# Two transpose banks kept through the attention, and a pair's sum and casts one step later

## The chip, the cores and the metric

The kernel runs on one core of a Trainium2 chip. The metric is device time in microseconds (us), the median of several runs. Its engines are called PE (TensorE matmul; PEld is its weight load), DVE (VectorE), ACT (ScalarE), POOL (GpSimd) and SP (SyncE, which issues most DMAs).

## The reference

Attention with hashed buckets over 2 x 8 heads of 768 positions and 64 dimensions, then two feed-forward blocks on the 1536 x 512 result:

```python
q_bits = (einsum(q, proj) > 0); k_bits = (einsum(k, proj) > 0)   # 6 bits each
mask = q_bucket[..., :, None] == k_bucket[..., None, :]          # same 6 bits
scores = where(mask, scale * q @ k.T, -1e9)
attn = softmax(scores)
x = attn @ v                                  # then (1536 x 512)
x = (sigmoid(x @ w_gate) * (x @ w_val)) @ w_out     # d_ff 1536
h = x @ w_in                                  # d_ff 2048
out = (h * cos(h)) @ w_out2
```

## The kernel before

Nearly every product is made of float32 values split in a rounded part and the rest, in two or three matmuls. `attention()` runs first and `moe()` behind it.

The attention is a software pipeline over steps `g`. A step is one head and one tile of 128 queries, so a head has T = 6 steps and all 16 heads have NG = 96. The stages of one step lie several steps apart: `scores` (PE, L483 and L486: the code bits and the values of q and k) writes the scores `s`; `rowmax` (DVE, L500) makes `mn`; `expo` (ACT, L507) makes the exponentials `p`, and after every third step `sm` (L517); `coef` (DVE, L533) makes the reciprocal `r`; `norm` (POOL, L540) scales `p`. LAG = 7 steps behind, `ptrans` (PE, L556) transposes blocks `t` of `p`, two to a step; `phi` (ACT, L561) rounds each to `ph`, `plo` (DVE, L566) makes the rest `pl`, and `pv` (PE, L576 with `ph`, L577 with `pl`) sums six of them into the output `o` of half a head. `fin_act` (ACT, L586) copies that one bank `o` to `e`; this comes every third step, and the first `pv` of the next half head can only follow it.

Two heads make a pair with 128 rows. When its last half is copied, DMAs bring its halves to the right partitions (L597 to L600), and then the pair is finished: `fin_sum` adds the two halves in `ef` (L613), `fin_hi` rounds the sum to the input `xy` of the feed-forward block (ACT, L625 or L642), `fin_lo` makes the rest (POOL, L646). For the first six pairs the sum is split: `fin_wide` adds 512 columns on DVE and rounds them on ACT (L625), while POOL adds the other 256, which `fin_hi` rounds (L642). SUM_AT, HIGH_AT and LOW_AT say how many steps after the copy of the pair's last half this is done (the sum on DVE and its cast one step after SUM_AT).

The next heads are prepared beside that: `trans` transposes q and k (`pt`, PE L302; rounded into `x`, or copied to `xf` by ACT, L319), `bits_steps` multiplies them by the projection in six matmuls (`pb`, PE L368), and `code` (DVE, L353) makes the code bits `bf`, which DMAs (L390) bring into the operands of `scores`.

The order on every engine is the order in which the code calls these functions, since the whole lies in a manual schedule: the lists ORDER, ROOM (steps with a wide sum), LAST and FILL (the steps before the first transposes of `p`) name the stages of a step in their order. PREP stands for what was put down for this step in advance (`todo`), S for the scores of a later step, FIN for the copy of `o`, SUM for `fin_wide`.

PSUM has eight banks. Scores take four; at the start another two hold a third buffer for scores, and two (`ps_u`) hold transposes and bits in turn. At step 5 `change_banks` gives these four back and makes three banks for `t`, `pt` and `pb` (`ps_t`) and one for `o` (`ps_o`). The feed-forward blocks begin with `pg`, `pv` and `ph` (L864), of which some fill PE at the end of the attention.

Of the kernel before, what the change touches and what calls it, by code (L numbers as in the profile page):

```python
# [9 lines left out]
F32 = mybir.dt.float32  # L10
# [6 lines left out]
PSUM = bass.MemoryType.PSUM  # L17

P = 128

ORDER = (
    "Tb LOa COEF NRM PVb EXP Ta MIN LATE W HIb PVa PREP S FIN HIa Tc PVaF LOb".split()
)
# [2 lines left out]
)  # L26
LAST = ["COEF", "NRM"] + [name for name in ORDER if name not in ("COEF", "NRM")]
FILL = "COEF NRM MIN EXP LATE W PREP S".split()

LOAD_AT = {"q": -17, "k": -19, "v": -6}  # L30
TRANS_AT = (-12, -10)
BITS_AT = -8
VALUES_AT = (-3, -1)

SUM_AT, HIGH_AT, LOW_AT = 3, 5, 5
BIG = float(2.0**34)
CUT = float(2.0**30)
INV2PI = 1.0 / (2.0 * math.pi)
# [5 lines left out]
def lsh_attention_glu_moe_cos_moe(  # L44
# [14 lines left out]
    B, H, S, D = q.shape  # L59
# [7 lines left out]
    HS = S // 2  # L67
# [168 lines left out]
    def attention():  # L236
        nonlocal done
        parts = None
        with ExitStack() as st:
# [4 lines left out]
            tiny = st.enter_context(tc.tile_pool(name="tiny", bufs=3))  # L244
            work = st.enter_context(tc.tile_pool(name="work", bufs=2))
            ps_s = st.enter_context(tc.tile_pool(name="ps_s", bufs=1, space=PSUM))
            first = ExitStack()
            ps_f = first.enter_context(tc.tile_pool(name="ps_f", bufs=1, space=PSUM))
            ps_t = first.enter_context(tc.tile_pool(name="ps_u", bufs=2, space=PSUM))
            ps_o = None  # L250

            def change_banks():
                nonlocal ps_t, ps_o
                first.close()
                s_ps.pop()
                ps_t = st.enter_context(tc.tile_pool(name="ps_t", bufs=3, space=PSUM))
                ps_o = st.enter_context(tc.tile_pool(name="ps_o", bufs=1, space=PSUM))

            NG = NH * T
            heads = {}  # L260
# [28 lines left out]
            def trans(hd, half, fast=False):  # L289
                hh = heads.setdefault(hd, {})  # L290
                if half == 0:
                    hh["x"] = [
                        prep.tile([P, T, P], F32R, tag=f"x{i}", name=f"x{i}_{hd}", bufs=2)
                        for i in range(2)
                    ]
                    for nm in ("q1", "k1", "q2", "k2"):
                        hh[nm] = prep.tile([P, T, P], F32R, tag=nm, name=f"{nm}_{hd}")
                xh, xl = hh["x"]
                sl = slice(3 * half, 3 * half + 3)
                pt = ps_t.tile([P, 3, P], F32, tag="t", name=f"pt{hd}{half}")  # L300
                for i in range(3):
                    nc.tensor.transpose(pt[:, i, :], raw[hd][:, 3 * half + i, :], ident)  # L302

                def high():
                    nc.scalar.activation(xh[:, sl, :], pt, AF.Copy, scale=qscale)

                def low():
                    nc.vector.scalar_tensor_tensor(
                        out=xl[:, sl, :],
                        in0=pt,  # L310
                        scalar=qscale,
                        in1=xh[:, sl, :].bitcast(F32),
                        op0=ALU.mult,
                        op1=ALU.subtract,
                    )

                def whole():
                    xf = work.tile([P, 3, P], F32, tag="xf", name=f"xf{hd}{half}", bufs=2)
                    nc.scalar.activation(xf, pt, AF.Copy, scale=qscale)  # L319
                    return xf  # L320

                def rest_of(xf):
                    nc.gpsimd.tensor_tensor(
                        out=xl[:, sl, :], in0=xf, in1=xh[:, sl, :].bitcast(F32), op=ALU.subtract
                    )

                def both():
                    xf = whole()
                    nc.gpsimd.tensor_scalar(
                        out=xh[:, sl, :], in0=xf, scalar1=1.0, scalar2=1.0, op0=ALU.mult, op1=ALU.mult  # L330
                    )
                    rest_of(xf)
                    if half == 1 and hd > 2:
                        place(hd, 0)
                        place(hd, 1)

                if hd == 1 and half == 0:
                    return high, lambda: rest_of(whole())
                return (high, low) if fast else both

            def place(hd, i):
                lo, hi = slice(0, D), slice(D, P)
                if i == 0:
                    raw.pop(hd)
                hh = heads[hd]
                for nm, rows, part in (
                    (("q2", slice(32, 96), lo), ("k1", lo, hi), ("q1", lo, lo), ("k1", hi, hi)),
                    (("k2", slice(32, 96), hi), ("q1", hi, lo)),
                )[i]:
                    nc.sync.dma_start(hh[nm][rows].bitcast(F32), hh["x"][i][part].bitcast(F32))  # L350
# [9 lines left out]
                )  # L360

            def bits_steps(hd):
                pb = ps_t.tile([P, HS], F32, tag="t", name=f"pb{hd}")
                hh = heads[hd]
                n = 0
                for low, half in ((0, 0), (0, 1), (1, 0), (1, 1)):
                    for i in range(2 - low):
                        nc.tensor.matmul(  # L368
                            pb,
                            pw[:, i, slice(0, P) if half else slice(D, D + P)],  # L370
                            hh["x"][low][:, 3 * half : 3 * half + 3, :],
                            start=(n == 0),
                            stop=(n == 5),
                        )
                        n += 1
                    yield pb
# [24 lines left out]

            def first_head():
                split = [trans(0, half, fast=True) for half in range(2)]
                hh = heads[0]
                xh, xl = hh["x"]
# [144 lines left out]

            def ptrans(w):
                u, j = divmod(w, T)
                pt = ps_t.tile([P, 3, P], F32, tag="t", name=f"t{w}")
                for i in range(3):
                    pv_ = p_t[3 * u + i].rearrange("p a s -> p (a s)")
                    nc.tensor.transpose(pt[:, i, :], pv_[:, j * P : (j + 1) * P], ident)  # L556
                pt_t[w] = pt
# [90 lines left out]
            LAG = 7  # L648
# [10 lines left out]
            for hd in range(2, NH):  # L659
                s1 = T * hd  # L660
                if hd > 2:
                    for nm in "qk":
                        at(max(s1 + LOAD_AT[nm], -2) if hd > 3 else 2, lambda hd=hd, nm=nm: load(hd, nm))
                if hd % 2 == 0:
                    at(max(s1 + LOAD_AT["v"], 8), lambda hd=hd: load(hd, "v"))
                for half in range(2):
                    if hd > 2:
                        at(
                            max(s1 + TRANS_AT[half], 7),
                            lambda hd=hd, half=half: trans(hd, half),  # L670
                        )
                    else:
                        at(3 * half - 1, lambda half=half: second_head(half))
                if hd > 2:
                    at(s1 + BITS_AT, lambda hd=hd: bits(hd))
                at(s1 + VALUES_AT[hd % 2], lambda hd=hd: values(hd))
# [12 lines left out]
            at(4, lambda: two_more())  # L689
            at(5, lambda: bits(2, split2[0])())  # L690
            at(5, change_banks)

            def second_head(half):
                if half == 0:
                    return trans(2, 0)
                high, low = trans(2, 1, fast=True)

                def upper():
                    high()
                    low()  # L700
                    place(2, 0)
                    place(2, 1)
                    split2.append(bits_steps(2))
                    next(split2[0])

                return upper
# [11 lines left out]
            with tc.manual_schedule(  # L718
# [35 lines left out]
                scores(0)  # L754
                scores(1)
                split1 = bits_steps(1)
                for _ in range(2):
                    next(split1)
# [10 lines left out]
                for g in range(NG + LAG + 2):  # L769
# [32 lines left out]
                    if g == LAG - 2:  # L802
                        at(g, lambda: ptrans(0))
                        at(g, lambda: ptrans(1))
# [21 lines left out]
                        "SUM": (g in wide, lambda: wide.pop(g)()),  # L826
                        "HIa": (0 <= wa + 2 < NW, lambda: phi(wa + 2)),
                    }
                    steps = ORDER if LAG - 1 <= g != NG else LAST if g == NG else FILL
                    for name in ROOM if g in wide else steps:  # L830
                        on, fn = ops[name]
                        if on:
# [5 lines left out]
    def moe():  # L838
        with ExitStack() as st:
# [172 lines left out]
            with tc.manual_schedule(  # L1012
# [8 lines left out]
                for n, (kind, l, f, c) in enumerate(items):  # L1021
# [7 lines left out]
                    else:  # L1029
                        (layer_out1 if l == 1 else layer_out2)(c, f)  # L1030

    attention()
    moe()

# [40 lines left out]
```

## Time and profile before

| what | value |
|---|---|
| median of 3 runs | 799.45 us (799.36 to 799.46) |
| the profiled execution | 800.5 us |
| span of the profiled execution | 798.7 us |
| granted TensorE clock | full (all 40 slices) |
| PE, PEld busy | 99%, 85% of the span |
| DVE, ACT, POOL busy | 64%, 59%, 40% |
| PE's own waits by releaser, above 0.1 us | 3.6 (first loads), 1.6, 1.0, 0.9, 0.3, 0.2 |

A timeline row gives the start in us, the duration, the engine and line, what is written from what, the shape and the count, and in brackets the idle time before it with what released it. Instructions of PE are pipelined: the next one can begin before the listed end of the last. The span of the attention is about the first 240 us.

### The profile page before, as it was taken

The page shows a single profiled execution, that of the slowest core. Times are in us where ns is not written, and L with a number is a line of the kernel's source. Part 1 is how long each engine was busy: PE and PEld are TensorE (multiplying, and loading weights), DVE is VectorE, ACT ScalarE, POOL GpSimd, SP SyncE. Part 2 cuts the span into 40 slices and gives each one's busy share as a digit, 9 for nine tenths or more (in the row PEclk, how much of TensorE's full clock was granted, in tenths as well). Part 3 has the DMA queues.
Part 4 walks back from the last instruction along what each step waited for, and adds up shares of the span by engine and source line. Part 5 has one row for each costly group of instructions (what it writes and reads, how often), then busy time and mean ns, then how long its engine had stood idle before and what let it go on. Part 6 is the DMA issues. An engine that isn't in the chain of part 4 may idle for free.

```text
span 798.7 us, 11638 instructions
## 1 busy us (share of the span) xinstructions
PE 787.3 (99%) x3984; PEld 677.8 (85%) x3984; DVE 511.2 (64%) x800; ACT 468.7 (59%) x931; POOL 321.5 (40%) x350
## 2 busy tenths in 40 slices
PE   6999999999999999999999999999999999999998
PEld 5999899999998888888888888888888888888886
DVE  7888898988985443334443266657655666676662
ACT  7899899999985333222332244456666656664442
POOL 6879888988871222222222112221222122222221
PEclk9999999999999999999999999999999999999999
DMA  7866675688413432222221122323223333242312
GB/s 174 195 155 148 161 172 142 152 206 202 116 49 100 132 116 94 80 80 79 80 80 53 53 79 80 119 67 121 90 80 105 106 106 98 87 157 81 105 53 105
DMA packets 70891, 89.03 MB, mean 111 GB/s; under 512 B 30129, under 2 KB 55089, under 8 KB 70833
## 3 DMA queue, kind: packets, MB, share of 16 engines
q1 hardware_dynamic: 67504, 85.30, 37.6%
q10 hardware_dynamic: 3328, 3.00, 1.3%
q8 instruction: 31, 0.51, 0.3%
q14 instruction: 28, 0.22, 0.1%
HBM read 59.77 MB, written 3.15 MB: 79 GB/s over the span
## 4 chain that ended last, share of the span: by engine, by line
PE 97%; DMA 1%; DVE 1%; ACT 1%; issue 0%; DVEq 0%; ACTq 0%
PE ph L864 16%; PE a L981 16%; PE pg L864 12%; PE pv L864 12%; PE a L926 12%; PE t L556 8%; PE o L576 4%; PE o L577 4%; PE s L483 4%; PE s L486 4%; PE pb L368 2%; PE pt L302 1%; PE a L957 1%; DMA k<-x 1%; DMA nqk<-in_k 0%; DVE mn L500 0%
## 5 line engine op out<-in xcount | busy, mean ns | idle before, releaser
L864 PE MATMUL ph<-xy,ih 128*128 128x512 f32 x384 | 118.3, 389 | 0.0
L132 ACT CAST gh<-g 128x512 fp32r<-128x512 f32 x84 | 52.1, 620 | 109.1 <-PE a L981 43.7
L566 DVE TENSOR_TENSOR pl<-t,ph 128x384 fp32r<-128x384 f32 x192 | 102.8, 553 | 13.1 <-ACT ph L561 11.0
L133 POOL TENSOR_TENSOR zl<-w_z,zh 128x512 fp32r<-128x512 f32 x32 | 41.5, 1295 | 167.0 <-ACT zh L132 167.0
L540 POOL TENSOR_SCALAR p<-p,r,d 128x768 f32<-128x768 f32 x96 | 97.6, 1021 | 22.0 <-PE s L486 7.7
L890 DVE TENSOR_TENSOR g<-pv,sg 128x512 f32<-128x512 f32 x36 | 24.9, 692 | 119.9 <-PE pv L864 119.9
L561 ACT CAST ph<-t 128x384 fp32r<-128x384 f32 x192 | 90.5, 484 | 14.3 <-PE t L556 12.5
L500 DVE TENSOR_REDUCE mn<-s 128x1 f32<-128x770 f32 x96 | 91.2, 950 | 10.7 <-PE s L486 9.2
L556 PE MATMUL t<-ident,p 128*128 128x128 f32 x576 | 93.7, 272 | 2.7 <-DVE r L533 1.6
L133 DVE TENSOR_TENSOR gl<-g,gh 128x512 fp32r<-128x512 f32 x84 | 57.8, 688 | 53.1 <-ACT gh L132 50.9
L507 ACT ACTIVATE p<-s,mn 128x768 f32<-128x768 f32 x96 | 87.9, 916 | 4.1 <-DVE mn L500 3.5
L864 PE MATMUL pg<-xy,gh 128*128 128x512 f32 x288 | 89.2, 390 | 0.0
L864 PE MATMUL pv<-xy,vh 128*128 128x512 f32 x288 | 88.6, 389 | 0.0
L888 ACT ACTIVATE sg<-pg 128x512 f32<-128x512 f32 x36 | 21.4, 593 | 112.7 <-PE pg L864 112.6
L864 PEld LDWEIGHTS ph<-xy,ih 128*128 128x128 f32 x384 | 72.1, 188 | 15.1
L556 PEld LDWEIGHTS t<-ident,p 128*128 128x128 f32 x576 | 74.4, 140 | 10.0 <-POOL vs L286 1.8
L576 PE MATMUL o<-ph,vs 128*128 128x384 f32 x192 | 78.5, 409 | 0.0
L864 PE MATMUL ph<-xy,il 128*128 128x512 f32 x192 | 74.7, 389 | 0.0
L981 PE MATMUL a<-zh,gl 128*128 128x512 f32 x184 | 71.7, 390 | 0.0
L981 PE MATMUL a<-zl,gh 128*128 128x512 f32 x184 | 71.6, 389 | 0.0
L981 PE MATMUL a<-zh,gh 128*128 128x512 f32 x184 | 71.6, 389 | 0.0
L483 PE MATMUL s<-k,q 96*128 96x384 f32 x192 | 69.1, 360 | 0.2 <-DVE q L353 0.2
(118 smaller groups left out, 1748.0 us busy)
## 6 DMA issues: line engine op xcount, KB each, us to landing
raw_z<-in_moe_w_out SPq DMA_DIRECT2D x32, 512.0 KB, 3.3
raw_o<-in_moe_w_out SPq DMA_DIRECT2D x23, 512.0 KB, 3.2
q<-x SPq DMA_DIRECT2D x45, 192.0 KB, 3.8
k<-x SPq DMA_DIRECT2D x45, 192.0 KB, 3.7
raw_i<-in_moe_w_in SPq DMA_DIRECT2D x16, 512.0 KB, 4.0
raw_g<-in_moe_w_gate SPq DMA_DIRECT2D x10, 512.0 KB, 3.5
raw_v<-in_moe_w_val SPq DMA_DIRECT2D x10, 512.0 KB, 3.5
nv<-in_v SPq DMA_DIRECT2D x8, 384.0 KB, 4.3
```

Of the source, the lines that this page charges most:

```text
L133: sub.tensor_tensor(out=dst_l, in0=src, in1=dst_h.bitcast(F32), op=ALU.subtract)
L483: nc.tensor.matmul(o, hh["q2"][0:96, t, :], hh["k2"][0:96, sl, :], start=True, stop=False)
L500: nc.vector.tensor_reduce(mn_t[u][:, i : i + 1], s_t[g][:, :, 0 : HS + 1], axis=AX.XY, op=ALU.min)
L507: nc.scalar.activation(pt, s_t.pop(g)[:, :, 0:HS], AF.Exp, bias=mn_t[u][:, i : i + 1], scale=-1.0, accum_out=sm_t[u][:, i : i + 1],)
L540: nc.gpsimd.tensor_scalar(out=pt, in0=pt, scalar1=r[:, i : i + 1], scalar2=d[:, i : i + 1], op0=ALU.mult, op1=ALU.add,)
L556: nc.tensor.transpose(pt[:, i, :], pv_[:, j * P : (j + 1) * P], ident)
L561: nc.scalar.copy(ph, pt_t[w])
L566: nc.vector.tensor_tensor(out=pl, in0=pt_t.pop(w), in1=ph_t[w].bitcast(F32), op=ALU.subtract)
L576: nc.tensor.matmul(o_t[u], vs[:, j, :], ph_t.pop(w), start=(j == 0), stop=False)
L864: nc.tensor.matmul(ps, w[:, kt, :], xy[c][:, hl, kt, :], start=(n == 0), stop=(n == 11))
L926: nc.tensor.matmul(acc[c, e], w[:, e, :], m, start=(f == 0 and n == 0), stop=(f == F1 - 1 and n == 2),)
L981: nc.tensor.matmul(acc[c, t], m[:, ts], w, start=(f == 0 and n == 0), stop=(f == F2 - 1 and n == 2),)
```

## The change

It has three parts. Two banks for transposes and bits (`ps_t`) are made at the start and kept, so that `change_banks` only has to make a third one (`ps_x`) and the one for `o`; `t_tile` gives every third block after that to `ps_x`. In steps 4 and 5 the list FILL_END puts the scores ahead of PREP. And a pair's sum, its casts and its rests come one step later.

```diff
+FILL_END = "COEF NRM MIN EXP LATE W S PREP".split()
-SUM_AT, HIGH_AT, LOW_AT = 3, 5, 5
+SUM_AT, HIGH_AT, LOW_AT = 4, 6, 6
...
+            ps_t = st.enter_context(tc.tile_pool(name="ps_t", bufs=2, space=PSUM))
             first = ExitStack()
             ps_f = first.enter_context(tc.tile_pool(name="ps_f", bufs=1, space=PSUM))
-            ps_t = first.enter_context(tc.tile_pool(name="ps_u", bufs=2, space=PSUM))
-            ps_o = None
+            ps_x = ps_o = None
+            blocks = 0
             def change_banks():
                 first.close()
                 s_ps.pop()
-                ps_t = st.enter_context(tc.tile_pool(name="ps_t", bufs=3, space=PSUM))
+                ps_x = st.enter_context(tc.tile_pool(name="ps_x", bufs=1, space=PSUM))
                 ps_o = st.enter_context(tc.tile_pool(name="ps_o", bufs=1, space=PSUM))
+            def t_tile(shape, name):
+                nonlocal blocks
+                if ps_x is not None:
+                    blocks += 1
+                pool = ps_x if blocks % 3 == 2 else ps_t
+                return pool.tile(shape, F32, tag="t", name=name)
...
-                pt = ps_t.tile([P, 3, P], F32, tag="t", name=f"t{w}")
+                pt = t_tile([P, 3, P], f"t{w}")
...
-                    steps = ORDER if LAG - 1 <= g != NG else LAST if g == NG else FILL
+                    steps = ORDER if LAG - 1 <= g != NG else LAST if g == NG else FILL_END if g >= 4 else FILL
```

`pt` and `pb` are taken from `t_tile` in the same way. Lines of the attention stand 9 further down in the changed kernel. In the rows below a name ends in the number of the buffer or of the writing.

On PE, around the last bits (`pb`) of head 2 in steps 4 and 5, before (`s_99` are the scores of step 6, `s_100` of step 7, further down):

```order
L368 MATMUL pb_303<-x_2_228,pw 128x384 x4
L368 MATMUL pb_303<-x_2_229,pw 128x384
L483 MATMUL s_99<-k_1_192,q_1_191 128x384
L486 MATMUL s_99<-k_1_190,q_1_189 128x384
L483 MATMUL s_99<-k_1_192,q_1_191 128x384
L486 MATMUL s_99<-k_1_190,q_1_189 128x384
L368 MATMUL pb_303<-x_2_229,pw 128x384
L556 MATMUL t_344<-ident,p_243 128x128
```

and now:

```order
L377 MATMUL pb_303<-x_2_228,pw 128x384 x2
L492 MATMUL s_99<-k_1_192,q_1_191 128x384
L495 MATMUL s_99<-k_1_190,q_1_189 128x384
L492 MATMUL s_99<-k_1_192,q_1_191 128x384
L495 MATMUL s_99<-k_1_190,q_1_189 128x384
L377 MATMUL pb_303<-x_2_228,pw 128x384 x2
L377 MATMUL pb_303<-x_2_229,pw 128x384
L492 MATMUL s_100<-k_1_192,q_1_191 128x384
L495 MATMUL s_100<-k_1_190,q_1_189 128x384
L492 MATMUL s_100<-k_1_192,q_1_191 128x384
L495 MATMUL s_100<-k_1_190,q_1_189 128x384
L377 MATMUL pb_303<-x_2_229,pw 128x384
```

Both blocks of scores moved ahead of the bits that are multiplied in the same step; the first transposes `t` follow the last `pb` in both, and the block `s_100` stood behind two of them.

On DVE, around the wide sum of the third pair, which the rows of the trace show between 117 and 122 us, before:

```order
L613 TENSOR_TENSOR ef_1600<-e_1477,ef_1600 128x512
L500 TENSOR_REDUCE mn_1984<-s_99 128x1
L353 TENSOR_SCALAR bf_1987<-pb_1945,bcode 128x384
L566 TENSOR_TENSOR pl_2005<-t_1966,ph_1993 128x384
L566 TENSOR_TENSOR pl_2011<-t_1978,ph_2003 128x384
L533 RECIPROCAL r_2013<-sm_1864 128x3
L500 TENSOR_REDUCE mn_1984<-s_100 128x1
```

and now:

```order
L509 TENSOR_REDUCE mn_1980<-s_99 128x1
L362 TENSOR_SCALAR bf_1983<-pb_1944,bcode 128x384
L575 TENSOR_TENSOR pl_2002<-t_1964,ph_1989 128x384
L575 TENSOR_TENSOR pl_2008<-t_1976,ph_2000 128x384
L542 RECIPROCAL r_2010<-sm_1863 128x3
L622 TENSOR_TENSOR ef_1599<-e_1475,ef_1599 128x512
L509 TENSOR_REDUCE mn_1980<-s_100 128x1
```

The sum went from ahead of one row maximum to ahead of the next one, behind the reciprocal.

On ACT, for the same pair, from the cast of the wide sum (`xy_69`) over that of the short one (`xy_70`) to the copy of `o`, before:

```order
L517 ACTIVATE sm_1864<-sm_1864,small 128x3
L625 CAST xy_69<-ef_1600 128x512
L561 CAST ph_1993<-t_1966 128x384
L561 CAST ph_2003<-t_1978 128x384
L507 ACTIVATE p_2020,sm_1985<-s_99,mn_1984 128x768
L561 CAST ph_2027<-t_2007 128x384
L642 CAST xy_70<-ef_1600 128x256
L561 CAST ph_2048<-t_2022 128x384
L507 ACTIVATE p_2061,sm_1985<-s_100,mn_1984 128x768
L319 ACTIVATE xf_2068<-pt_2037,qscale 128x384
L561 CAST ph_2072<-t_2052 128x384
L586 COPY e_1957<-o_1961 128x384
```

and now:

```order
L526 ACTIVATE sm_1863<-sm_1863,small 128x3
L570 CAST ph_1989<-t_1964 128x384
L570 CAST ph_2000<-t_1976 128x384
L516 ACTIVATE p_2017,sm_1981<-s_99,mn_1980 128x768
L634 CAST xy_69<-ef_1599 128x512
L570 CAST ph_2026<-t_2004 128x384
L570 CAST ph_2044<-t_2019 128x384
L516 ACTIVATE p_2057,sm_1981<-s_100,mn_1980 128x768
L328 ACTIVATE xf_2064<-pt_2036,qscale 128x384
L570 CAST ph_2068<-t_2048 128x384
L651 CAST xy_70<-ef_1599 128x256
L595 COPY e_1955<-o_1959 128x384
```

The cast of 512 columns moved behind the exponential of the next step, and that of 256 columns from between two roundings to right ahead of the copy. Past the attention's last steps, two or three `pg` matmuls come earlier on PE, and the seventh pair's two casts stand ahead of a copy on ACT.

## Rows read from the trace of the kernel before

**Rows 1.** The page's first part: busy time, share of the span, instructions.
```profile
PE 787.3 (99%) x3984; PEld 677.8 (85%) x3984; DVE 511.2 (64%) x800; ACT 468.7 (59%) x931; POOL 321.5 (40%) x350
```

**Rows 2.** PE's waits by releaser: us in total, times, longest.
```profile
PE t L556 <- DVE r L533: 1.6, 1, 1.6
```

**Rows 3.** Timeline of PE, 15 to 24 us.
```profile
17.44 0.34 PE L483 MATMUL s<-k,q 96*128 96x384 f32 x1
...
18.16 0.34 PE L368 MATMUL pb<-x,pw 128*128 128x384 f32 x1
...
23.13 0.44 PE L577 MATMUL o<-pl,vs 128*128 128x384 f32 x1 [0.31 <-DVE pl L566]
```

**Rows 4.** Timeline of SP's queue, 14 to 16 us.
```profile
14.90 1.23 SPq L390 DMA_DIRECT2D q<-bf  x2
```

**Rows 5.** DMA issues at 14.9 us: count, KB, us to landing.
```profile
q<-bf SPq DMA_DIRECT2D x1, 48.0 KB, 2.3
```

**Rows 6.** Timeline of DVE, 18 to 23.5 us.
```profile
19.23 0.67 DVE L353 TENSOR_SCALAR bf<-pb,bcode 128x384 fp32r<-128x384 f32 x1
...
21.65 0.96 DVE L500 TENSOR_REDUCE mn<-s 128x1 f32<-128x770 f32 x1 [1.66 <-PE s L486]
22.52 0.55 DVE L566 TENSOR_TENSOR pl<-t,ph 128x384 fp32r<-128x384 f32 x1
```

**Rows 7.** Timeline of all engines, 89 to 92.5 us, the second pair.
```profile
89.67 0.96 DVE L613 TENSOR_TENSOR ef<-e,ef 128x512 f32<-128x512 f32 x1 [1.48 <-DMA q<-x]
...
92.14 0.55 PE L556 MATMUL t<-ident,p 128*128 128x128 f32 x3 [1.03 <-DVE bf L353]
```

**Rows 8.** Timeline of DVE, 114 to 126 us, the third pair.
```profile
117.63 0.70 DVE L613 TENSOR_TENSOR ef<-e,ef 128x512 f32<-128x512 f32 x1
...
120.79 0.93 DVE L500 TENSOR_REDUCE mn<-s 128x1 f32<-128x770 f32 x1
```

**Rows 9.** Timeline of ACT, 114 to 126 us, the same pair.
```profile
118.36 0.62 ACT L625 CAST xy<-ef 128x512 fp32r<-128x512 f32 x1
...
119.61 0.48 ACT L561 CAST ph<-t 128x384 fp32r<-128x384 f32 x1 [0.20 <-PE t L556]
119.98 0.91 ACT L507 ACTIVATE p<-s,mn 128x768 f32<-128x768 f32 x1
...
120.99 0.48 ACT L561 CAST ph<-t 128x384 fp32r<-128x384 f32 x1
121.37 0.41 ACT L642 CAST xy<-ef 128x256 fp32r<-128x256 f32 x1
121.68 0.48 ACT L561 CAST ph<-t 128x384 fp32r<-128x384 f32 x1
122.05 0.91 ACT L507 ACTIVATE p<-s,mn 128x768 f32<-128x768 f32 x1
...
122.94 0.59 ACT L319 ACTIVATE xf<-pt,qscale 128x384 f32<-128x384 f32 x1
123.44 0.48 ACT L561 CAST ph<-t 128x384 fp32r<-128x384 f32 x1
123.82 0.49 ACT L586 COPY e<-o 128x384 f32<-128x384 f32 x1
```

**Rows 10.** Timeline of PE, 114 to 127 us: the next half head's first `o`.
```profile
124.58 0.33 PE L576 MATMUL o<-ph,vs 128*128 128x384 f32 x1
```

**Rows 11.** Timeline of all engines, 214.5 to 216.2 us: a copy and what follows.
```profile
215.18 0.50 ACT L586 COPY e<-o 128x384 f32<-128x384 f32 x1
...
215.73 0.44 PE L576 MATMUL o<-ph,vs 128*128 128x384 f32 x1
...
216.01 0.34 PE L577 MATMUL o<-pl,vs 128*128 128x384 f32 x1
```

**Rows 12.** Timeline of POOL, 114 to 127 us.
```profile
117.60 1.50 POOL L540 TENSOR_SCALAR p<-p,r,d 128x768 f32<-128x768 f32 x1
...
119.79 0.99 POOL L540 TENSOR_SCALAR p<-p,r,d 128x768 f32<-128x768 f32 x1
```

More of the change, by code (lines that the diff above doesn't have):

```diff
@@ L246, in attention @@
             ps_s = st.enter_context(tc.tile_pool(name="ps_s", bufs=1, space=PSUM))
+            ps_t = st.enter_context(tc.tile_pool(name="ps_t", bufs=2, space=PSUM))
             first = ExitStack()
             ps_f = first.enter_context(tc.tile_pool(name="ps_f", bufs=1, space=PSUM))
-            ps_t = first.enter_context(tc.tile_pool(name="ps_u", bufs=2, space=PSUM))
-            ps_o = None
+            ps_x = ps_o = None
+            blocks = 0
             def change_banks():
-                nonlocal ps_t, ps_o
+                nonlocal ps_x, ps_o
                 first.close()
                 s_ps.pop()
-                ps_t = st.enter_context(tc.tile_pool(name="ps_t", bufs=3, space=PSUM))
+                ps_x = st.enter_context(tc.tile_pool(name="ps_x", bufs=1, space=PSUM))
                 ps_o = st.enter_context(tc.tile_pool(name="ps_o", bufs=1, space=PSUM))
+            def t_tile(shape, name):
[4 more added lines that the diff above has]
+                return pool.tile(shape, F32, tag="t", name=name)
             NG = NH * T
@@ L299, in trans @@
                 sl = slice(3 * half, 3 * half + 3)
-                pt = ps_t.tile([P, 3, P], F32, tag="t", name=f"pt{hd}{half}")
+                pt = t_tile([P, 3, P], f"pt{hd}{half}")
                 for i in range(3):
@@ L362, in bits_steps @@
             def bits_steps(hd):
-                pb = ps_t.tile([P, HS], F32, tag="t", name=f"pb{hd}")
+                pb = t_tile([P, HS], f"pb{hd}")
                 hh = heads[hd]
```

## The prediction

> **What bounds the kernel now.** I read the busy shares first: PE is busy 99% of the span, DVE 64%, ACT 59% and POOL 40% [rows 1]. A change that only reorders work can then win no more than the idle time of PE that it removes. So the second view is the list of PE's own waits; a transpose behind DVE's reciprocal `r` is the longest that this change can reach, 1.6 us [rows 2]. The third view is the timeline around the places where an instruction changes its row. It tells what the busy shares hide: inside the attention ACT works back to back, each instruction beginning 0.10 us before the listed end of the last (121.37 + 0.41 against 121.68 [rows 9]), so what ACT does between two evacuations of the one `o` bank sets how late the second one is.
>
> **First part: the start (banks and FILL_END).** The block of scores of step 6 moves ahead of three `pb` matmuls, the block of step 7 ahead of the last `pb`. Step 6's block can't begin before its code bits arrive: the two q<-bf transfers are issued at 14.90 [rows 4] and land 2.3 later [rows 5], at 17.2. It began at 17.44 and took 0.72, up to the `pb` at 18.16 [rows 3]; it stays where it is. Then three `pb` at 0.18 (the 0.72 is four matmuls), the block of step 7 (0.72) and the last `pb`: it ends at about 19.7, where it ended at 18.16 + 0.34 = 18.5. So `bf`, on DVE at 19.23, comes at 19.73, a loss of 0.5 on that chain; the time for step 7's block comes out of the 1.6 that PE waited for its first transposes [rows 2]. But the row maximum of step 7, which waited 1.66 for scores and began at 21.65 [rows 6], now stands behind `bf` and the short reciprocal, at 19.73 + 0.67 = 20.40, so it is 1.25 earlier. Behind it the first `pl`, at 22.52 [rows 6], comes at 21.27, and the `o` matmul that waited for it, at 23.13 [rows 3], at 21.88. From there PE has no gap to give: **gain 1.25**. Its bounds are 0.9 (two places of 0.18 more ahead of the last `pb`, if the transfer lands later) and 1.9 (with the 0.31 that this `o` had to wait and one matmul's 0.34 of restart).
>
> **Second part: the second pair's sum.** The sum `ef` on DVE waited 1.48 for a transfer and took 0.96; behind it on DVE stood the row maximum and `bf`, and PE's transpose waited 1.03 for that `bf` at 92.14 [rows 7]. One step later the transfer has landed, the row maximum and `bf` no longer stand behind the sum, and the wait goes. Nothing else is late there: the row maximum was the only other one behind it. With 0.16 for the restart (PE's next matmul follows 0.18 after the last one's begin, where 0.34 of it count as busy) the **gain is 1.2**, bounds 1.0 and 1.4.
>
> **Third part: the sum, the casts and the `o` bank.** This is where I expect the price. Six pairs are summed by `fin_wide` and six later evacuations `e` follow them. I work one out, between 117 and 125 us.
> On DVE the sum was at 117.63 and took 0.70; it now stands behind the reciprocal, where the next row maximum began at 120.79 [rows 8], so it runs from 120.79 to 121.49 (and that row maximum 0.70 later, still ahead of the exponential that needs it). On ACT the 512-column cast ran at 118.36, at a place where ACT had time to spare (the second rounding behind it, at 119.61, still waited 0.20 for its transpose [rows 9]). Now the cast stands behind the exponential that ends at 119.98 + 0.91 = 120.89 and waits there for the sum: it starts at 121.52, and ACT is idle for 0.6. Behind it, in ACT's order, each at the distance that the rows of before show for the same two neighbours: rounding at 122.04 (was 120.99), rounding at 122.42 (was 121.68, the short cast between them being gone), exponential 122.79 (was 122.05), `xf` 123.68, rounding 124.18, and then, new in this place, the 256-column cast at 124.56 with 0.31 to the next. So the evacuation `e` runs from 124.87 to 125.36, where it began at 123.82 and ended at 124.31 [rows 9].
> PE's first `o` of the next half head needs that one bank. It ran at 124.58 [rows 10], 0.27 after the evacuation. How near it can come is seen where it was already the limit: the copy at 215.18 + 0.50, the matmul at 215.73, 0.05 later [rows 11]. So it now runs at 125.41, **0.83 late**, plus 0.10, since the next matmul follows a restart by 0.28 (215.73 to 216.01) and not by 0.18. I take 0.9 for each pair, bounds 0.6 (half of the 0.6 of idle ACT regained) and 1.15 (the 1.05 of the evacuation with the restart and no slack at all). Part of it may be shown as a wait of a transpose for `pl`, which is late by the same chain; it's the same time. The sixth pair lies at a step in which ACT and DVE also prepare a weight piece; I give it the same. **Loss 6 x 0.9 = 5.4**, bounds 3.6 and 6.9.
> POOL's part of the sum is one normalization later and its rests one step later; nobody waits for those before the MoE. SP's queue keeps its order.
>
> **Fourth part: the run-out.** The seventh pair's two casts now stand ahead of an evacuation too, and two or three gate matmuls that filled PE there come earlier. Between nothing (they cover each other) and 0.6 (both casts, 0.62 and 0.41, less their covered part); near the lower end, since there the gate matmuls can still be between: **loss 0.2**.
>
> **The sum.** -1.25 - 1.2 + 5.4 + 0.2 = **+3.15 us**. The profiled span is 798.7 us, so 801.85; the median of the runs shown, 799.45, is 0.75 above that span, which gives **802.6 us** for the median.
>
> **The rivals.**
> *Faster: the order on ACT and DVE is free.* PE is 99% busy and the others are not [rows 1], so all of the third part could be hidden and only the two gains be left: 799.45 - 2.45 = 797.0. Against it stand ACT's back-to-back rows and the 0.27 between evacuation and matmul [rows 9, 10]: the move costs as soon as it makes the evacuation more than 0.22 later. The Trainium skill says in "Perfetto Trace Analysis", Identifying the Most-Contended Engine and Identifying Performance Opportunities, that one finds the engine with the highest occupancy and that gains come from it; taken by itself this rule speaks for this rival, at 797.0; of the third part the busy shares that it reads say nothing.
> *No change: only the short cast counts.* If the wait of the long cast is made up by later gaps, what is left is the 256-column cast's 0.31 ahead of the evacuation, less the 0.22 of slack, with its restart: about 0.19 a pair, 1.1 in all, and 799.45 - 2.45 + 1.1 = 798.1. Against: between 120.99 and 124.31 ACT shows no gap to make it up in.
> *Slower still: the sum meets POOL.* The sum of the second pair took 0.96 where the other took 0.70 [rows 7, 8], and a normalization on POOL beside the latter took 1.50 where one without took 0.99 [rows 12]. In its new place the sum runs beside a normalization again; if it is the one that is held, 0.26 a pair, 1.6 in all: 804.2. The Trainium skill, "SBUF — State Buffer", section "SBUF: two separate sides", has VectorE and GpSimd share a port that one of them holds alone while the other stands still; the two long rows agree with that, and its reading that the loser stands fully still would make the time this one.
> *The banks do nothing.* If step 7's scores are held by something that I don't see, the first gain is 0: 803.85.
>
> **How the numbers follow.** Forecast 0.70, faster 0.11, no change 0.07, the sum held by POOL 0.07, no gain at the start 0.05. A measurement of this kernel can tell about 0.2% (1.6 us) from no change, so "same" is 797.85 to 801.05. The forecast's lower bounds (3.6 for the loss, full gains) reach into it, for which I put 0.11 of its 0.70. Faster 0.11, same 0.07 + 0.11 = 0.18, slower 0.59 + 0.07 + 0.05 = 0.71. For the range I leave out the faster rival and the no-change rival, together 0.18: it begins at 799.45 - 1.9 - 1.2 + 3.6 = 799.95, rounded down to 799.8, and ends at 805.0, which takes in the last two rivals and 0.4 a pair over the forecast (802.6 + 2.4).
>
> **What would show it.** In the profile after, PE's waits should list an `o` behind ACT's `e`, six times or so and some 0.8 each (or a part of it as `t` behind `pl`); ACT's 512-column cast should have an idle time of about 0.6 behind DVE's `ef`; the 1.0 behind `bf` should be gone; the `o` that was at 23.13 should be near 21.9. If there is no wait for `e`, the third part is wrong and the first rival right. If there are such waits but the 512-column cast starts without idle time, the sum was not the cause, and if `o` is still near 23.1, the first part is wrong.

## The result

The changed kernel takes 803.78 us (median of 6 runs, 803.59 to 805.06), the kernel before 799.46 us (6 runs, 799.36 to 801.28): a ratio of 1.0051, 95% interval 1.0041 to 1.0062. It is slower, 1.2 us more so than the 802.6 of the prediction, and within its range. The profiled execution of the changed kernel took 803.59 us and has a span of 801.8 us, where the prediction's sum made 801.85.

The first part of the page after, beside [rows 1]: PE's busy share is 99% as before, and its busy time is 3.0 us longer.

```profile
PE 790.3 (99%) x3984; PEld 677.6 (85%) x3984; DVE 510.3 (64%) x800; ACT 468.4 (58%) x931; POOL 320.2 (40%) x350
```

PE's waits after (us in total, times, longest), to be read beside [rows 2]:

```profile
PE pt L311 <- DMA nqk<-in_k: 3.8, 1, 3.8
PE s L492 <- DMA q<-bf: 1.4, 1, 1.4
PE o L585 <- ACT e L595: 1.4, 5, 0.3
PE s L492 <- DVE q L362: 0.2, 1, 0.2
PE o L586 <- DVE pl L575: 0.2, 1, 0.2
```

The waits behind `r` (1.6) and `bf` (1.0) are gone, another at the start (1.4 behind `q<-bf`) has come, and five waits of `o` for ACT's copy `e` are new. PE's listed waits are together no longer than before, though the span is 3.1 us longer. A listed idle time of PE is only what lies beyond the end of the last matmul as the profile shows it, and that end overlaps the next start by 0.16 in normal running (0.34 long, the next after 0.18); a delay of 0.3 can so be shown as 0.1 or as nothing, and then stands in the busy time. The five waits for `e` are listed with at most 0.3, where the prediction looked for some 0.8 or a part of it. What a place costs is read better from the start of the same matmul in the two traces.

The place that the prediction worked out, the third pair, after. ACT first (start, duration, what it does, in brackets the idle time before it and its releaser), beside [rows 9]:

```profile
119.36 0.91 ACT L516 ACTIVATE p<-s,mn 128x768 f32<-128x768 f32 x1
120.16 0.20 ACT L516 ACTIVATION_READ_ACCUMULATOR p<-s,mn 128x1 f32 x1
120.87 0.62 ACT L634 CAST xy<-ef 128x512 fp32r<-128x512 f32 x1 [0.51 <-DVE ef L622]
121.39 0.85 ACT L570 CAST ph<-t 128x384 fp32r<-128x384 f32 x2
122.14 0.92 ACT L516 ACTIVATE p<-s,mn 128x768 f32<-128x768 f32 x1
...
123.02 0.59 ACT L328 ACTIVATE xf<-pt,qscale 128x384 f32<-128x384 f32 x1
123.48 0.49 ACT L570 CAST ph<-t 128x384 fp32r<-128x384 f32 x1
123.84 0.44 ACT L651 CAST xy<-ef 128x256 fp32r<-128x256 f32 x1
124.15 0.51 ACT L595 COPY e<-o 128x384 f32<-128x384 f32 x1
```

DVE in the same stretch, beside [rows 8]:

```profile
120.10 0.16 DVE L542 RECIPROCAL r<-sm 128x3 f32<-128x3 f32 x1
120.18 0.66 DVE L622 TENSOR_TENSOR ef<-e,ef 128x512 f32<-128x512 f32 x1
120.76 0.95 DVE L509 TENSOR_REDUCE mn<-s 128x1 f32<-128x770 f32 x1
121.90 1.02 DVE L575 TENSOR_TENSOR pl<-t,ph 128x384 fp32r<-128x384 f32 x2 [0.19 <-ACT ph L570]
```

And PE, beside [rows 10]:

```profile
122.07 0.34 PE L495 MATMUL s<-k,q 128*128 128x384 f32 x1
122.51 0.55 PE L565 MATMUL t<-ident,p 128*128 128x128 f32 x3
...
124.12 0.33 PE L495 MATMUL s<-k,q 128*128 128x384 f32 x1
124.72 0.44 PE L585 MATMUL o<-ph,vs 128*128 128x384 f32 x1 [0.26 <-ACT e L595]
125.00 0.34 PE L586 MATMUL o<-pl,vs 128*128 128x384 f32 x1
```

Up to this place the changed kernel is 0.62 us ahead: the long cast's neighbour, the exponential at 119.98 of before, begins at 119.36. The long cast waits 0.51 for the sum, the copy starts at 124.15, 0.33 later than before, and `o` follows its end (124.66) by 0.06, where before it had 0.27. The transposes at 122.51 follow the scores by 0.44 and not 0.18: they use the bank of the block three before, which the first `pl` of the row at 121.90 still reads. PE's list has no wait for it, but the row of the weight load names it:

```profile
122.51 0.31 PEld L565 LDWEIGHTS t<-ident,p 128*128 128x128 f32 x3 [0.42 <-DVE pl L575]
```

So this pair delays PE in two pieces, at `t` and at `o`. The `o` that was at 124.58 is at 124.72, so 0.62 ahead has become 0.14 behind, and the restart adds 0.10 (125.00 is 0.28 after it, not 0.18): 0.86 lost, of which 0.33 stood at `t` and 0.53 at `o`. None of the six pairs costs less than 0.8.

### The profile page after: what moved, and what is told of

It is laid out like the page before. It is cut to its first block, busy times and chain, and to the rows that moved or that the text cites. A ratio compares the mean times of both kernels' runs of the same rounds, so it can differ in the third digit from the quotient of the medians.

```text
span 801.8 us, 11669 instructions
## 1 busy us (share of the span) xinstructions
PE 790.3 (99%) x3984; PEld 677.6 (85%) x3984; DVE 510.3 (64%) x800; ACT 468.4 (58%) x931; POOL 320.2 (40%) x350
## 4 chain that ended last, share of the span: by engine, by line
PE 92%; ACT 3%; DVE 2%; issue 1%; DMA 1%; SPq 0%; DVEq 0%; ACTq 0%
PE ph L873 16%; PE a L990 16%; PE pg L873 12%; PE pv L873 12%; PE a L935 12%; PE t L565 6%; PE o L585 4%; PE o L586 3%; PE s L492 3%; PE s L495 3%; PE pb L377 2%; PE pt L311 1%; ACT p L516 1%; PE a L966 1%; ACT ph L570 1%
## 5 line engine op out<-in xcount | busy, mean ns | idle before, releaser
L549 POOL TENSOR_SCALAR p<-p,r,d 128x768 f32<-128x768 f32 x96 | 95.7, 1004 | 20.9 <-PE s L495 7.6
```

Of the source, the lines that this page charges most:

```text
L549: nc.gpsimd.tensor_scalar(out=pt, in0=pt, scalar1=r[:, i : i + 1], scalar2=d[:, i : i + 1], op0=ALU.mult, op1=ALU.add,)
```

## The experiments

All times are medians; each ratio is to runs of the kernel before on the same chip and at the same time. The loss of one pair in a run is always the same reckoning: the start of the same PE matmul in this trace and in that of the kernel with the start alone (e1), before and after the pair.

### The kernel before, again

> The kernel before, unchanged, once more, for the spans of its single executions. The medians differ by 4.3 us and the two profiled spans by 3.1. Theory: the wait of PE for bf at 92 us (1.03, with its restart 1.25) is not in most executions of the kernel before; it was in the profiled one because a transfer landed late there. Then most executions have a span near 797.6 and a time near 799.45, some have spans 1 to 2 us longer, and a profile whose span is near 797.6 shows no wait for bf near 92 us. Rival: the wait is in every execution, and the difference lies outside the span; then every span is near 798.7, at 799.45 as well.

Measured: 799.52 us, 11 runs between 799.19 and 801.29. Of the 27 comparison runs beside it 18 are between 799.29 and 799.77 (spans 797.5 to 798.0) and 9 between 800.6 and 801.04 (spans 798.8 to 799.2). The profile has a span of 797.6 and no wait for `bf`. Its DVE rows at the second pair, against [rows 7]:

```profile
88.30 0.71 DVE L613 TENSOR_TENSOR ef<-e,ef 128x512 f32<-128x512 f32 x1
88.99 0.96 DVE L500 TENSOR_REDUCE mn<-s 128x1 f32<-128x770 f32 x1
89.87 0.67 DVE L353 TENSOR_SCALAR bf<-pb,bcode 128x384 fp32r<-128x384 f32 x1
```

The sum waits for nothing, since its transfer landed in time. The DMA issues at 82.4 us of this trace, and at 82.9 us of the trace shown ahead of the prediction (KB, us to landing):

```profile
e<-e SPq DMA_DIRECT2D x1, 192.0 KB, 5.2
```

```profile
e<-e SPq DMA_DIRECT2D x1, 192.0 KB, 6.3
```

The bracket in [rows 7] names `q<-x`, but the first `q<-x` issued behind it landed at 90.1, when the sum (89.67) had begun; the landing that fits is that of `e<-e`, at 89.2.

The theory holds: the wait was in the execution profiled first and is not in the usual one. Whether the executions near 800.7 and above have this wait was not seen, and their clock speaks for another cause, which stays open: they all list a mean granted clock of 0.995 to 0.998, those below 800 and the profiled one with the wait (800.5) list 0.999 or 1.000.

Nor is a late transfer confined to that one execution. Of the eight traces with the sum in its early place (before, this one, e1 and e6 to e10), four have one wide sum that waits for its transfer: 1.48 in the trace shown first, 0.87 in e9, 0.41 in e6, 0.40 in e8. Behind them PE lost about 1.25, 0.37, 0.22 and nothing. In the five traces with the sum one step later no wide sum waits. So the later sum gains something in executions with a late transfer; in the medians no gain is seen.

### The start alone

```diff
-SUM_AT, HIGH_AT, LOW_AT = 4, 6, 6
+SUM_AT, HIGH_AT, LOW_AT = 3, 5, 5
```

(an edit of the changed kernel, as the others where nothing else is said)

> The first two parts of the change alone (two banks kept, scores ahead of the bits in steps 4 and 5), with SUM_AT, HIGH_AT, LOW_AT back at 3, 5, 5. Theory: the first o behind pl comes 1.1 us earlier than before and nothing of that is given back: 798.3 us (797.9 to 798.8), no wait for an o bank behind e. Rival: the gain at the start is lost again at the first place where ACT limits PE: 799.4.

Measured: 798.37 us, ratio 0.9983 (0.9974 to 0.9992). As the theory said, 1.13 us less than the kernel before, and PE's list of waits has only two entries left:

```profile
PE pt L311 <- DMA nqk<-in_k: 3.8, 1, 3.8
PE s L492 <- DMA q<-bf: 1.3, 1, 1.3
```

### The later sum alone

```diff
-SUM_AT, HIGH_AT, LOW_AT = 3, 5, 5
+SUM_AT, HIGH_AT, LOW_AT = 4, 6, 6
```

(an edit of the kernel before)

> The third part alone (SUM_AT, HIGH_AT, LOW_AT 4, 6, 6), with the banks and the lists of before. Theory: six times 0.83 to 0.94 of loss, nothing else: 799.45 + 5.4 + 0.1 = 804.9 us (804.4 to 805.4), five or six waits of o for ACT's e of about 0.3 and as many restarts of transposes behind pl; less the 1.25 of the second pair if that wait is in every execution of before: 803.7. Rival (the loss needs the new banks, whose third block has one buffer alone): about 799.5.

Measured: 804.97 us, ratio 1.0066 (1.0053 to 1.0079). 5.47 us lost; with the 1.13 of the start this makes 4.34, and the whole change measured 4.32. So the two parts add up, and the 1.25 of the second pair is not in the medians.

### Both casts in the gaps of later steps

```diff
+WIDE_AT, CAST_AT = 4, (7, 10)
+SUM_AT, HIGH_AT, LOW_AT = 3, 5, 5
...
+                                for n, c in zip(CAST_AT, (512, 256)):
+                                    casts[g + n] = lambda u=fin, c=c: fin_hi(u, c)
+                                    at(g + n + 1, lambda u=fin, c=c: fin_lo(u, c))
+                                return
```

> The changed kernel with another place for the casts: the sum stays one step later for the six wide pairs (written into e, so that ef is free again), but ACT's 512-column cast comes in the next step with a gap (3 steps behind the old place), the 256-column cast in the one after that, the rests on POOL one step behind each; the last pairs are finished as before the change. Theory: the loss was ACT's idle wait for the sum ahead of the copy of o, so it goes altogether: no wait of o for e, no idle time of ACT behind ef, 798.3 us or a little less (797.0 to 798.6). Rival: it is the later sum on DVE that costs (it holds up the row maximum), wherever the casts stand: 801 to 803.8.

Measured: 801.11 us, ratio 1.0015 (1.0006 to 1.0024). The theory's time is missed, and the measured one lies at the low end of the rival's range: 2.7 us of the loss are gone, 2.7 remain, 0.43 to 0.49 in each of the first five pairs. ACT no longer waits for the sum, and no `o` waits for `e`. What is left is seen in two rows of ACT's timeline and one of DVE's:

```profile
121.05 0.90 ACT L517 ACTIVATE p<-s,mn 128x768 f32<-128x768 f32 x1 [0.20 <-DVE mn L510]
...
124.77 0.60 ACT L649 CAST xy<-e 128x512 fp32r<-128x512 f32 x1
```

```profile
125.78 1.02 DVE L576 TENSOR_TENSOR pl<-t,ph 128x384 fp32r<-128x384 f32 x2 [0.68 <-ACT ph L571]
```

The exponential now waits 0.20 for a row maximum that stands behind the sum on DVE, and the long cast isn't free in its new step either: the roundings behind it hold up `pl` by 0.68, and PE's transposes after that start 0.21 late. So I took the loss apart further.

### The long cast without its wait

```diff
-                        nc.scalar.copy(h, x)
+                        lo, hi = wide_cols(u, True)
+                        nc.scalar.copy(h, e_t[u // 2 - 1][:, lo:hi])
```

> The changed kernel, but the 512-column cast of the wide pairs rounds the first summand e in place of the sum, so that it waits for nothing (its output is not the pair's sum there); the sum itself runs on DVE as in the changed kernel. Theory: what costs is ACT's idle time behind the sum (0.51 in the profile, some 0.6 with the overlap); without it the copy of o is 0.6 earlier and the loss of a pair falls from 0.85 to 0.2 to 0.45 (the upper end if the sum on DVE has a price of its own, as the casts in gaps showed 0.4 a pair): 799.8 to 801.1 us. Rival: the order and the work on ACT alone count, the idle time would be there anyway: 803.8.

Measured: 801.46 us, ratio 1.0016 (1.0007 to 1.0025); 0.51 to 0.54 a pair in the first five. Less than the 803.8 of the rival, more than I gave it. At the third pair the delay at `t` is gone (0.33 in the changed kernel), and of the 0.53 at `o` 0.49 are left. So what the wait for the sum adds is the delay at `t`, through `pl` and the bank of a transpose; `o` is nearly as late without it. The row that explains this is again an exponential behind the row maximum:

```profile
119.62 0.62 ACT L635 CAST xy<-e 128x512 fp32r<-128x512 f32 x1
120.12 0.87 ACT L570 CAST ph<-t 128x384 fp32r<-128x384 f32 x2
121.17 0.90 ACT L516 ACTIVATE p<-s,mn 128x768 f32<-128x768 f32 x1 [0.17 <-DVE mn L509]
```

ACT now has its time back, and spends a part of it waiting for DVE. Five waits of `o` for `e` remain, at most 0.2.

### The casts late, the sum early

```diff
+SUM_AT, HIGH_AT, LOW_AT = 3, 6, 6
...
+                                casts[g + SUM_AT + 2] = lambda u=fin: fin_cast(u)
```

> The changed kernel with the sum back in its old place on DVE and POOL (SUM_AT 3) and both casts on ACT in the places of the changed kernel. Theory: the sum is long done when its cast comes, so ACT does not idle, and DVE's row maximum is not held up: 798.4 + 6 x 0.25 = 799.9 us (799.3 to 800.6); o waits for e by little or not at all. Rival: the casts' new place costs it all, sum or no sum: 803.8. The difference to the run whose cast reads e is the price of the sum's place on DVE alone: about 0 if it has none, some 1 to 2 us in all if the casts in gaps were right.

Measured: 800.31 us, ratio 1.0003 (0.9994 to 1.0012); 0.23 to 0.26 a pair from the second to the fifth, 0.62 at the first, 0.37 at the sixth. No wait of `o` for `e` is listed. In the profiled execution the first pair's sum met a late transfer, which cost PE 0.22 of the 0.62 before `o`:

```profile
59.30 1.00 DVE L622 TENSOR_TENSOR ef<-e,ef 128x512 f32<-128x512 f32 x1 [0.41 <-DMA q<-x]
```

The difference to the last run is 1.15 us in the medians and 0.26 to 0.30 in each pair from the second to the fifth. It is the price of the sum's place, which that run and this one differ in (and in what the long cast reads).

### The short cast late, alone

```diff
-SUM_AT, HIGH_AT, LOW_AT = 4, 6, 6
+SUM_AT, HIGH_AT, LOW_AT = 3, 6, 6
```

> The start of the changed kernel, the sum and the 512-column cast in their old places, only the 256-column cast right ahead of the copy of o (SUM_AT, HIGH_AT, LOW_AT 3, 6, 6). Theory: 0.31 ahead of a copy with 0.22 to spare costs 0.09 and a restart of 0.10 a pair: 798.4 + 1.1 = 799.5 us. Rival: the roundings ahead of it are earlier by as much, so the copy is where it was: 798.4 (798.1 to 798.7).

Measured: 799.80 us, ratio 0.9997 (0.9988 to 1.0006), 1.43 more than the start alone (which ran on another chip; the profiled spans differ by 1.5): 0.20 in each of the first five pairs, 0.36 at the sixth, and 0.16 in the run-out. The theory's 799.5 is 0.3 short, and the rival's 798.4 falls. The rows at the third pair, ACT and then PE:

```profile
121.93 0.41 ACT L651 CAST xy<-ef 128x256 fp32r<-128x256 f32 x1
122.24 0.48 ACT L595 COPY e<-o 128x384 f32<-128x384 f32 x1
```

```profile
122.52 0.33 PE L495 MATMUL s<-k,q 128*128 128x384 f32 x1
122.77 0.45 PE L585 MATMUL o<-ph,vs 128*128 128x384 f32 x1
123.06 0.34 PE L586 MATMUL o<-pl,vs 128*128 128x384 f32 x1
```

The copy ends at 122.72, `o` follows 0.05 later, as in [rows 11]; it would have begun 0.18 after the scores, at 122.70. The delay is hardly seen as a wait: 0.07 at `o` and 0.11 at its successor (123.06).

### The short cast back between the roundings

```diff
-SUM_AT, HIGH_AT, LOW_AT = 4, 6, 6
+SUM_AT, HIGH_AT, LOW_AT = 4, 5, 6
```

> The changed kernel with HIGH_AT 5 again: the 256-column cast stands between the two roundings of the step before and no longer right ahead of the copy of o (SUM_AT 4, LOW_AT 6 as changed). Theory: ACT has no idle time between its wait for the sum and the copy, so it does not matter where in this stretch the short cast stands: 803.8 us (803.4 to 804.4, rather longer, since one rounding and the pl behind it come later). Rival: the place right ahead of the copy is what costs: 6 x 0.31 less, 801.9.

Measured: 804.87 us, ratio 1.0058 (1.0046 to 1.0071), 1.07 to 1.16 us in each of the first five pairs, where the changed kernel has 0.85 to 0.89. The rival falls, and the theory's range is passed. At the third pair the two pieces at `t` and at `o` are as in the changed kernel (0.33 and 0.52): for these it doesn't matter where the short cast stands, as the theory said. The rest comes some 4 us later, at a transpose that waits for POOL:

```profile
128.09 0.99 POOL L549 TENSOR_SCALAR p<-p,r,d 128x768 f32<-128x768 f32 x1
```

```profile
129.13 0.14 PEld L565 LDWEIGHTS t<-ident,p 128*128 128x128 f32 x1 [0.18 <-POOL p L549]
```

The short cast stands ahead of `xf` again, and POOL works on `xf` before this normalization; measured from the start of the pair's sum, both are 0.3 later than in the changed kernel, which has no such wait. It is listed in four of the first five pairs. The place that is dear by itself is the cheaper one here.

### The parts of the start

Two banks alone:

```diff
-                    steps = ORDER if LAG - 1 <= g != NG else LAST if g == NG else FILL_END if g >= 4 else FILL
+                    steps = ORDER if LAG - 1 <= g != NG else LAST if g == NG else FILL
```

> The two kept banks alone: the list FILL in steps 4 and 5 as before, SUM_AT, HIGH_AT, LOW_AT 3, 5, 5. Theory: the first transposes of p no longer wait for the bits to leave their bank, so they and the scores of step 7 behind them start when the last third bank is free (about 19.2 us) and the row maximum of step 7 follows: 798.1 to 798.4 us, as good as with the lists. Rival (the lists make the gain): 799.4.

(numbers 3, 5, 5 here and in the next two.) Measured: 798.42 us, ratio 0.9980 (0.9971 to 0.9989).

The list alone is the edit of that line in the kernel before:

> FILL_END in steps 4 and 5 alone, with the banks and the numbers of before. Theory: all three banks for t come from change_banks and wait for the bits, which leave 0.5 later: the first transposes at about 20.5 and not 19.7; part of the gain is lost: 798.5 to 799.2 us. Rival (the banks do nothing): 798.4.

Measured: 798.84 us, ratio 0.9991 (0.9983 to 1.0000).

The list in step 5 only:

```diff
-                    steps = ORDER if LAG - 1 <= g != NG else LAST if g == NG else FILL_END if g >= 4 else FILL
+                    steps = ORDER if LAG - 1 <= g != NG else LAST if g == NG else FILL_END if g == 5 else FILL
```

> The two kept banks, FILL_END in step 5 alone, numbers 3, 5, 5. In step 4 three bits' matmuls then stand ahead of the scores of step 6 again and run while these wait for their code bits (1.3 us of PE's idle time), and the last bits come 0.4 earlier, with all that hangs on them. Theory: 798.0 us (797.8 to 798.3). Rival: the chain from the row maximum is not what ends last there: 798.4, as with the list in both steps.

Measured: 798.10 us, ratio 0.9979 (0.9970 to 0.9988). All three came as the theory said, the first at the edge of its range. With the list alone PE's first transposes wait until 20.84, with the banks alone they start at 18.51 (the first three) and 19.47:

```profile
20.84 1.17 PE L557 MATMUL t<-ident,p 128*128 128x128 f32 x9 [0.86 <-DVE r L534]
```

```profile
18.51 0.49 PE L565 MATMUL t<-ident,p 128*128 128x128 f32 x3
19.47 0.55 PE L565 MATMUL t<-ident,p 128*128 128x128 f32 x3 [0.47 <-ACT p L516]
```

The profile names `r`, which ends 0.08 behind `bf`, the reader of the bits' bank; which of the two releases the transposes is not told apart. The banks alone give as much as banks and lists together, since in step 4 the list takes three bits' matmuls out of the time in which PE waits for `q<-bf` (1.4 in the list of waits after). With the list in step 5 alone that time is used, and both scores still come early. In its median this kernel is 0.3 us faster than both others, though the intervals overlap. Its one trace shows the lead and its loss: its transposes are 0.25 to 0.4 ahead of those of the start alone from 19.2 to 34.2 us, and 0.2 behind from there on, since one waits for POOL:

```profile
34.49 0.33 PE L565 MATMUL t<-ident,p 128*128 128x128 f32 x1 [0.31 <-POOL p L549]
```

How often this wait occurs is not shown.

## Why the prediction was right, and where not

**What bounds.** PE bounds the kernel and its list of waits is where one begins, but of the losses of this change only a quarter stands in that list: five waits, 1.4 us, of some 5.3.

**First part, predicted -1.25: right.** Between the profiled executions the `o` that was at 23.13 comes at 22.00, 1.13 earlier; the start alone measured 1.13 in its median. Step 7's scores start at 18.79 and the last `pb` at 19.49, within 0.2 of the working. But the working gave the banks no term: it followed the order of the scores alone. With that order and without the banks (e9) step 7's row maximum is early too, at 20.69, but the transposes wait until 20.84, and the gain is 0.7. So what the working took as one part are two that don't add up: 1.13 by the banks, 0.7 by the lists, 1.13 by both. The rival in which the banks do nothing fell.

**Second part, predicted -1.2: right for the profiled execution, wrong for the median.** Against the trace of the start alone, the first trace of before loses 1.25 at that place. But the step "the median of the runs shown, 799.45, is 0.75 above that span" hid that the profiled execution of before, with 800.5, was 1.05 longer than the median through this wait: its `e<-e` took 6.3 us to land, in the second trace 5.2, and there the sum has nothing to wait for. Those 1.05 us were nearly the same as the 1.25 of this wait, and both stood in the text. This one term is the difference between 802.6 and 803.78; the errors of the other three (0.12, 0.14 and 0.05) cancel to less than 0.1.

**Third part, predicted 6 x 0.9: right in size, and in the chain for the most part.** Measured 0.85 in each of the first four pairs, 0.89 and 0.97 in the last two, 5.26 in all. At the third pair the row of each step came within 0.1 of the working once the 0.62 that this kernel is ahead there is taken off: sum 120.17 and 120.18, long cast 120.90 and 120.87, copy 124.25 and 124.15, `o` 124.79 and 124.72, idle time of ACT 0.6 and 0.51. What the working called one cause the runs took apart, adding one piece after another to the start alone, for a pair in the middle:

| added | run | loss of a pair | more by |
|---|---|---|---|
| short cast ahead of the copy | e7 | 0.20 | 0.20 |
| long cast behind the exponential | e6 | 0.24 | 0.04 |
| sum behind the reciprocal on DVE | e3 | 0.53 | 0.29 |
| long cast waits for the sum | changed kernel | 0.85 | 0.32 |

The wait for the sum, which I gave as the cause, is the largest piece but not the most of it, and in this order of adding its 0.32 stands at `t`, while the working had put the 0.83 at `o` and only allowed for a part at `t`. I had noted that the row maximum would be 0.70 later and "still ahead of the exponential that needs it". That was so with ACT held up by the cast; without that, the exponential waits for it. Which piece has which price also hangs on the order of adding: with the wait in place the short cast is cheaper in its new place than in the old one (e4).

**Fourth part, predicted 0.2: right.** In all runs with HIGH_AT 6 the first `o` of the run-out is 0.6 late, and some 0.45 of it is made good by the first `pv` matmuls of the feed-forward block, so 0.15 is lost; in the two with 5 there (e4, e5) nothing is lost.

**The rivals.** That ACT and DVE have room (797.0) fell with e2: shares of 59% and 64% over the span say nothing of a stretch in which ACT works without a gap. The rule of the Trainium skill ("Perfetto Trace Analysis", Identifying the Most-Contended Engine) names PE here, and the trace agrees that PE bounds, with 99%; by it alone the time would have been 797.0, and the measurement decides: 5.3 us were lost by moves on the two other engines. That only the short cast counts had the right price for it (0.19, measured 0.20) and was too small as a whole. That the sum is held by POOL fell too. In five of the six pairs the sum runs beside a normalization for its last 0.40, and in the third for 0.13; it took 0.66 in all six. It's POOL's instruction that is longer where they meet, 1.27 (1.53 in the sixth pair) against 0.98 in the third, and no wait of PE for it is listed. The second pair, DVE and POOL:

```profile
91.08 0.66 DVE L622 TENSOR_TENSOR ef<-e,ef 128x512 f32<-128x512 f32 x1
```

```profile
91.34 1.27 POOL L549 TENSOR_SCALAR p<-p,r,d 128x768 f32<-128x768 f32 x1 [0.44 <-PE t L565]
```

And POOL at the third:

```profile
120.71 1.95 POOL L549 TENSOR_SCALAR p<-p,r,d 128x768 f32<-128x768 f32 x2 [0.72 <-PE o L586]
```

The two sums that were long had POOL at work well before them: the 0.96 of [rows 7] began 0.33 after a sum on POOL, the 1.00 of e6 0.52 after a normalization.

## What to carry to other kernels

Where one engine is full and another works back to back ahead of the copy that frees its only bank, a step moved on that other engine has more prices than its own length: the idle time that it puts there (0.32 of the 0.85 here), what it makes a third engine late with (0.29), and its length beyond the slack of the copy (0.20 with the restart). Compare the start of the same matmul in two traces rather than the lists of waits: a third of a microsecond can be lost with none listed. And before a wait is taken for a gain, hold the profiled execution against the median: if it is longer by about that wait, as here by 1.05 for 1.25, the wait is probably not in the usual execution.

## What was not expected of the hardware

A transfer of 192 KB (`e<-e`) landed 6.3 us after its issue in one execution, 5.2 in another of the same kernel and 4.6 in the changed one; in the 13 traces the one of the second pair took 4.3 to 7.1. With 0.8 us between landing and use, as in the second trace of before, that decides whether DVE waits 1.48 or nothing. A restart of PE costs about 0.10 beyond the wait itself, in [rows 11] and in the rows of the changed kernel alike (0.28 from 124.72 to 125.00, and not 0.18). A wide sum that began 0.25 ahead of POOL's normalization took 0.66, and the normalization 1.27 and not 0.98; one that began 0.33 behind a sum on POOL took 0.96.
